# One planned kernel, two sets of ranks: a searched instruction order is replaced by another

## The chip, the cores and the metric

The kernel runs on one core of a Trainium2 chip. The time is device microseconds of one execution of the whole program. A core has engines that run beside each other, each with its own instruction queue that is worked off strictly in order: TensorE (PE, matrix products; its weight loads are listed as PEld), VectorE (DVE), ScalarE (ACT), GpSimd (POOL) and SyncE (SP), which here does nothing but issue transfers from memory. An engine waits for another by a semaphore.

## What is computed

Four layers follow each other over 2048 tokens of width 640: attention A, mixer B, attention A, mixer B, each with a normalization ahead of it and a residual sum. The same weights serve both A layers and both B layers.

```
A: for each of 64 segments of 32 tokens, in order:
     h = [mem (8 rows), normalized segment (32 rows)]
     q, k, v = h Wq, h Wk, h Wv                     # 32 heads of 192
     o = softmax(mask(q k^T / sqrt(192))) v Wo
     mem = o[:8]; out = o[8:]
B: h  = gelu(ln(x) w1), quarters of it shifted by +1, -1, +2, -2 tokens
   x1 = x + h w2;   out = x1 + gelu(ln(x1) w3) w4
```

The memory rows make attention a recurrence: a segment needs the memory that the segment before it left.

## The kernel before

Steps and lanes. The kernel runs both A layers at once. Lane 0 is a segment of the first A layer, lane 1 a segment of the second, five segments behind it (`LAG = 5`). There are 69 steps: steps 0 to 4 have lane 0 alone, 5 to 63 both lanes, 64 to 68 lane 1 alone. In a two-lane step the 2 x 40 rows of the two lanes stand side by side, so that a weight tile that is loaded once serves both. The B layers run in chunks of 64 tokens per lane, one chunk in every two steps, between the operations of the attention steps. A steady pattern is therefore a pair of steps. Most of the weights don't fit on chip and stream in again in every step.

Inside `attention_step` eight groups of four heads go through the same chain. `keys_queries` makes keys (psk) and queries (psq), L943; ScalarE copies the queries (qT, L954), and three copies bring the keys to kT: one by VectorE (L962), and two half-height ones, of which ScalarE has the one and VectorE the other (L969). `attend` then does, by names that the ranks use:

- `fs` (PE, L1059): scores into pss
- `f1` (DVE, L1071): adds the mask and takes the row minimum
- `f2` (ACT, L1078): exponential, into Pm
- `f3` (DVE, L1082, L1083, L1084): sums, reciprocals, the product with them
- `f4` (PE, L1094): transposes of Pm into pst
- `f5` (ACT, L1102): copy to PT
- `f6` (PE, L1111): PT times values, into pso
- `f7` (DVE L1124 and ACT L1122): copies of the two halves of pso to oT

`project` (`f8`, PE, L1146) multiplies each half of oT with Wo and sums into psy over the step. `values3` makes the values (psv, L999), four matmuls of 32 weight columns side by side (the 32-row mode; PE changes into and out of it); ScalarE copies them to V (L979), and `fst` (DVE, L1022) moves parts of V to and from a stash, because in every even step the values of a part of the next step are made too. At the end of a step the memory rows go from psy into the next step's input hT (`fm`, L1173, lane 0 by ScalarE, lane 1 by VectorE), and the other rows into yTB (L1181).

The chunk operations are on VectorE and ScalarE too: residual sums (L1344, L1519, L1626), statistics (L1192 and after), gelu (L1234 to L1247), and copies of transposed tiles; their matmuls are L1443, L1502, L1565 and L1611, their transposes L1216, L1332 and L1339. GpSimd computes the reciprocal roots (L1202, L1383) and moves small pieces and chunk rows.

What sets the order. Nothing is issued in the order in which the functions run. Each calls `add` with an engine, a planned duration, a due time, the function that issues the instructions, and the buffers that it reads and writes. From the buffers `add` makes the edges between operations. It also looks up a rank: `RANK` holds, for each kind of step (`first`, `step0`, `step1`, single-lane kinds with `a` and `b`, `chunk`, `chunk_end` and so on) and for each operation's name, one number for each occurrence; the operation's priority is the time at which its step begins plus this number. `STEP = 48` is the nominal length of a step.

`Plan.place` then places operation after operation. For each engine it takes those that could start within 0.12 us (PE) or 0.05 us (others) of the earliest, and of these the one of the lowest priority; then the engine whose choice starts first. It counts with these lines:

```
free[e] = o.end - (OVER if e in ("ACT", "DVE") else 0.0)
...
elif x.e == e:
    at = o.end
else:
    at = o.end + (PE_LAT if e == "PE" else LAT)
```

`OVER` is by how much an operation on VectorE or ScalarE may start before the end of the one ahead of it, `PE_LAT` and `LAT` are the time from the end of an operation to the start of one on another engine that needs it. Weight loads are in two streams (`wa` for attention, `wb` for the chunks), each sorted by due time, not by rank; both are issued by SyncE. A load for a ring buffer is held until the buffer is free, and many are paced: they wait for a matmul that the plan has finished by then. In the end the operations are issued in the order of the plan, so that each engine's queue has its operations in that order. The planned times themselves don't reach the chip; only the order and the waits do. An operation's waits are made from the tiles that it touches.

Of the kernel before, what the change touches and what calls it, by code (L numbers as in the profile page):

```python
# [21 lines left out]
HG = 4  # L22
# [13 lines left out]
HI = (4.0, 3.0, 0.5)  # L36
# [12 lines left out]
LAT = 0.12  # L49
PACE = 0.25  # L50
OVER = 0.07
PE_LAT = 0.3
# [17 lines left out]
        "apply_ln.f": (25.27, 41.664, -40.648,),  # L70
        "chunk.f1": (45.412,),
        "chunk.f2": (-82.555,),
        "chunk.f3": (3.327,),
        "chunk.fe": (24.593,),
        "chunk.fe3": (21.521,),
        "chunk.fel": (42.947,),
        "chunk.fh": (-0.422,),
        "chunk.fhr": (63.222,),
        "chunk.fhs": (50.947,),
        "chunk.fl": (28.336,),  # L80
        "chunk.fs": (-9.07, 87.616,),
        "chunk.ft": (7.491,),
        "chunk.ftl": (17.084,),
        "chunk.fw": (12.223, 22.504, -3.661, 53.412, 35.584, 12.252, 39.5, 46.586, 6.412, 58.779, 65.304, -26.695,
            70.326,),
        "chunk.fx": (-11.005,),
        "chunk.fx0": (22.308, -12.232,),
        "chunk.fxu": (56.045,),
        "chunk.fz": (56.767,),
        "gelu.f1": (38.422, 8.702, 36.115, -5.73, 21.831, 15.367, 64.826,),  # L90
        "gelu.f2": (43.173, 25.388, 24.176, 19.651, 26.845, 61.238, 13.188,),
        "gelu.f3": (22.801, 11.157, 6.781, 20.622, 53.105, 19.314, 93.475,),
        "gelu.f4": (10.721, 20.836, -33.181, 19.632, -36.914, 31.698, 22.735,),
        "ln_ops.f1": (11.17, 37.33,),
        "ln_ops.f2": (63.628, 7.618,),
        "load_b.fn": (65.723, 2.515, -5.69, 32.658, 14.841, 42.334, 13.103, 39.659, 31.513, 14.364, -26.748,
            28.991, -16.99,),
        "transposes.f": (-36.173, -13.388, 3.992,),
    },
    "chunk_end": {  # L100
        "apply_ln.f": (6.64,),
        "chunk_end.fc": (57.832, 24.612, 4.237,),
        "chunk_end.fs": (38.711, 43.074,),
        "chunk_end.fst": (95.595, 64.015,),
        "chunk_end.fw": (90.265, 22.799, 53.015, 46.575, 23.39, 90.769,),
        "chunk_loads.f": (-2.609, 25.49, 54.721, 25.49, 119.762,),
        "chunk_loads.fz": (93.177, 10.841,),
        "ln_ops.f1": (5.751,),
        "ln_ops.f2": (54.739,),
        "load_b.fn": (20.608, 39.141, 22.427, 3.097, 19.618, 38.065,),  # L110
        "transposes.f": (67.877,),
    },
    "first": {
        "attention_step.attend.f1": (17.516, 11.944, 14.226, 51.703, 15.679, 65.842, 19.995, -4.963,),
        "attention_step.attend.f2": (32.206, 42.804, 35.52, 41.913, -17.146, -14.377, 72.053, -27.992,),
        "attention_step.attend.f3": (-7.419, 21.341, -6.131, 6.53, 64.995, 69.729, 29.276, 10.119,),
        "attention_step.attend.f4": (10.251, 43.894, 9.208, 36.337, -7.089, -6.588, 28.677, 84.166,),
        "attention_step.attend.f5": (14.759, 3.778, -100.306, 53.388, 82.279, 0.476, 47.399, 15.365,),
        "attention_step.attend.f6": (90.867, 51.374, 14.829, -13.387, 17.139, -1.653, -11.48, 21.746,),
        "attention_step.attend.f7": (24.097, 32.506, -26.804, 15.046, 99.332, 15.074, 33.257, 0.473, 24.79, 21.819,  # L120
            44.274, 15.984, 46.8, -11.85, 91.331, -6.294,),
        "attention_step.attend.fs": (60.998, 29.267, -12.034, -20.909, -26.536, 49.498, 35.908, -49.275,),
        "attention_step.fm": (-61.879,),
        "attention_step.fy": (25.64,),
        "attention_step.keys_queries.fk": (17.421, 58.065, 9.482, 20.243, 9.394, -98.29, 7.011, 33.049,),
        "attention_step.keys_queries.fk2": (-4.397, 14.541, 0.117, 21.364, 22.853, -9.996, 51.371, 12.329, -0.942,
            20.9, 57.916, 6.956, 17.166, 53.786, -1.12, 2.359,),
        "attention_step.keys_queries.fn": (-13.958, -17.525, 11.691, -25.108, 33.6, 24.516, -1.859, 18.409, 24.831,
            40.038, -26.96, 38.663, -14.016, -41.294, 98.804, 16.239, -13.809, 19.397, 1.785, 82.684, -31.643,
            20.351, 48.626, 49.47, 62.456, -30.688, -19.311, 32.72, -1.817, -26.25, 56.128, 29.575, -8.583,  # L130
            -17.298, 29.27, 36.05, -13.413, 28.739, 22.805, 44.373, 33.733, 41.172, 59.995, 29.44, 19.316, -14.128,
            -42.971, -21.254, -22.334, 55.507, -26.092, 24.156, 37.618, 13.893, -32.471, -2.697, -8.536, -14.197,
            18.653, 29.426, 82.311, 4.407, 35.396, -56.925,),
        "attention_step.keys_queries.fq": (-13.353, 21.377, 42.471, -2.143, 80.272, 36.699, -4.403, -15.8,),
        "attention_step.project.f8": (37.543, -0.806, 26.185, -3.505, 34.604, 23.024, -14.191, 31.212, 4.164,
            1.038, -3.259, 37.652, -52.502, -35.229, -7.961, 59.829,),
        "attention_step.v_copy.fe": (19.654, -51.565, 21.646, -22.381, 22.407, 6.892, 38.736, 77.812, 14.575,
            -18.961, -28.987, 55.198, 4.611, 56.209, 9.831, 65.23,),
        "attention_step.values.fv": (-17.77, 20.626, 38.167, -40.002, 80.137, 64.626, 30.911, 32.6,),
        "load_pair.fn": (48.935, 59.468, 10.497, 32.661, 50.274, 37.547, 28.935, 9.775, 53.542, 46.99, 40.122,  # L140
            36.648, 112.97, 32.973, -92.931, 33.724, -11.929, -12.279, 42.521, 2.858, 56.922, 37.386, 26.098,
            14.743, 33.522, 13.106, -14.298, 13.674, -8.217, -0.55, 13.502, -8.22, 40.412, 66.89,),
        "res_tile.fn": (116.073, 26.692, 15.064, 6.014, 5.501, 33.759, 3.951, 78.07, 78.067, 29.286, 42.528,
            -1.231, 36.946, 18.179, 12.925, -20.94, 153.972, 45.562, 102.56, 44.042,),
    },
    "last": {
        "apply_ln.f": (15.55, 43.414, 24.403,),
        "chunk.fc2": (-35.922, 69.473,),
        "chunk.fhr": (81.736,),
        "chunk.fs": (16.778, 14.665,),  # L150
        "chunk.ft": (1.105,),
        "chunk.fw": (28.085, -24.907, -12.43, -4.473, 0.43, -1.158, -12.745, -45.377, -28.417, 8.666, 54.761,),
        "chunk.fx": (29.273,),
        "chunk.fxu": (23.382,),
        "chunk.fz0": (131.626,),
        "chunk.halves.fa": (87.746, 5.116,),
        "chunk.halves.fd": (1.941, -19.583,),
        "chunk.halves.fn": (26.898,),
        "gelu.f1": (-43.383, 77.058, 13.807, 6.784, 64.672, 16.189,),
        "gelu.f2": (-32.682, -1.806, -11.508, 4.099, 26.283, -24.627,),  # L160
        "gelu.f3": (51.44, 35.022, 19.314, 63.957, 22.411, 49.713,),
        "gelu.f4": (9.085, 9.082, 68.146, 24.736, 61.493, -21.618,),
        "ln_ops.f1": (-12.151, 16.761,),
        "ln_ops.f2": (19.688, 54.968,),
        "load_b.fn": (10.497, 39.223, 41.188, 36.31, 9.331, -26.904, -11.528, 106.685, 30.89, 11.853, 5.373,
            33.721, 40.049,),
        "transposes.f": (-21.635, 103.144,),
        "warm.fwarm": (34.071, 4.62, -30.566, -28.23, 41.493, 17.753, 22.802, 4.697, -30.894, -0.639, 15.017,
            -26.293, -11.758,),
    },  # L170
    "last_end": {
        "chunk_end.fs": (-1.799, 35.629,),
        "chunk_end.fst": (11.599, -16.415, 45.847, 23.719,),
        "chunk_end.fw": (-3.425, 18.9, -25.169, 39.823, 36.518, -23.839, 8.894, 1.265,),
        "load_b.fn": (27.538, 83.834, 26.762, 26.765, 24.871, 14.264,),
    },
    "start": {
        "apply_ln.f": (16.824,),
        "chunk_loads.f": (93.18, 44.689, 6.824,),
        "ln_ops.f1": (1.076,),  # L180
        "ln_ops.f2": (57.543,),
        "start.f1": (15.362,),
        "start.f2": (-2.19,),
        "start.f3": (-11.851,),
        "start.f4": (-11.213,),
        "start.f5": (34.327, 11.809, -2.229, 11.05,),
        "transposes.f": (31.955,),
# [408 lines left out]
def kernel(  # L596
# [296 lines left out]
    def attention_step(t):  # L893
# [88 lines left out]
        def values3(i_, pr, s0, wbs, wv):  # L982
# [33 lines left out]
            for j in range(2) if ahead_v or behind_v else ():  # L1016
# [7 lines left out]
                if behind_v:  # L1024
                    add("DVE", 0.46, s0, fst, r=(B("stash", pr, j),), w=(B("V", j, "s"),))
                else:
                    add("DVE", 0.46, s0 + 0.2, fst, r=vk_, w=(B("stash", pr, j),))
# [744 lines left out]
```

## Time and profile before

| | |
|---|---|
| median of 3 runs | 3314.65 us (3310.34 to 3320.3) |
| profiled execution, its own time | 3318.65 us |
| its span, first to last instruction | 3316.5 us |
| mean granted TensorE clock | 0.990 |
| busy: PE, PEld, DVE, ACT, POOL | 96%, 85%, 70%, 57%, 7% |
| from memory | 817.14 MB read, 248 GB/s over the span |

The span parts into three: about 256 us until the first two-lane step (of which the first step takes 89 us), 59 two-lane steps at 95.5 us a pair, and about 239 us for the five last steps and the last chunk. These come from the times of the copies at the end of each step (L1181).

How to read the profile: a row of a group names line, engine, operation and tiles. A busy share is that of the whole span. In the waits, `A <- B: total, times, longest` says that the engine of A sat idle until B had ended, in us. In a timeline row the columns are start, length, engine, line, operation, tiles and shapes, count, and in brackets the idle time ahead of it and what ended it. In windows the columns are the stretch, its length, the busy time of PE, PEld, DVE, ACT and POOL with instruction counts, the granted clock, the busy share of DMA and its GB/s. Records of matmuls overlap: each is some 200 ns long while they follow each other at a fraction of that. "Cover" in what follows is the PE work that stands in PE's queue between a matmul and a later one that needs its result through other engines.

### The profile page before, as it was taken

Reading aid. Unit: us, or ns where it says so; the run is one execution under the profiler, and the core shown is the slowest. Engines: PE = TensorE matmul, PEld = TensorE weight load, DVE = VectorE, ACT = ScalarE, POOL = GpSimd, SP = SyncE. Lnnn points to the kernel's source line nnn. Section 1 sums busy time; section 2 is a strip of 40 time slices with the busy share of each in tenths; the row PEclk is TensorE's granted clock in tenths of the full one; section 3 lists DMA queues with packets and bytes.
Section 4 is the critical chain, followed back from the end, with each engine's and each line's share of the span. In section 5 each row is a group of like instructions: output and inputs, shape, how many; then the busy total and the mean of one; then the engine's idle time right before and its main releaser. Section 6 shows DMA issues by size and latency. Waiting matters only on the chain.

```text
span 3316.5 us, 173787 instructions
## 1 busy us (share of the span) xinstructions
PE 3183.1 (96%) x77339; PEld 2809.2 (85%) x77341; DVE 2329.5 (70%) x7320; ACT 1898.7 (57%) x4837; POOL 235.1 (7%) x483
## 2 busy tenths in 40 slices
PE   6899999999999999999999999999999999999997
PEld 4778888888888888888888888888888888888875
DVE  2666777777777777777767777677777777777665
ACT  2346666666565666665656666565666655666443
POOL 0000000000000000000000000000000000000000
PEclk7999999999999999999999999999999999999999
DMA  9787778777877777777778777877777777778885
GB/s 374 263 275 246 235 242 267 237 234 252 270 233 238 263 248 232 238 264 259 236 235 273 236 228 251 268 237 236 262 247 234 236 263 254 236 238 271 277 268 198
DMA packets 409752, 833.66 MB, mean 251 GB/s; under 512 B 39680, under 2 KB 207311, under 8 KB 409000
## 3 DMA queue, kind: packets, MB, share of 16 engines
q1 hardware_dynamic: 401704, 809.47, 72.8%
q0 software_dynamic: 7136, 13.00, 1.3%
q8 instruction: 605, 9.91, 1.2%
q14 instruction: 147, 1.20, 0.1%
q10 hardware_dynamic: 160, 0.08, 0.0%
HBM read 817.14 MB, written 5.24 MB: 248 GB/s over the span
## 4 chain that ended last, share of the span: by engine, by line
PE 71%; DVE 20%; DMA 3%; issue 3%; ACT 2%; SPq 0%; POOL 0%; ACTq 0%; DVEq 0%; POOLq 0%
PE psy L1146 15%; PE psk L943 14%; PE psq L943 13%; PE psv L999 10%; PE pss L1059 3%; PE pso L1111 3%; PE y L1611 3%; PE pst L1094 3%; DVE Pm L1084 2%; DVE sm L1082 2%; DVE oT L1124 2%; PE psh L1565 2%; DVE kT L962 2%; DVE st L1192 2%; DVE pss L1071 2%
## 5 line engine op out<-in xcount | busy, mean ns | idle before, releaser
L943 PEld LDWEIGHTS <-wst 128*128 128x128 bf16 x19872 | 804.2, 99 | 78.5 <-issue 62.1
L1146 PE MATMUL psy<-oT,wo 128*128 128x80 bf16 (+1 forms) x16560 | 701.8, 200 | 33.3 <-DVE oT L1124 11.3
L1146 PEld LDWEIGHTS <-wo 128*128 128x128 bf16 x16560 | 631.6, 99 | 75.5 <-issue 63.6
L979 ACT CAST V<-psv 96x384 bf16<-96x384 f32 (+3 forms) x1264 | 583.1, 473 | 119.2 <-PE psv L999 54.5
L943 PE MATMUL psq<-hT,wst 128*128 128x80 bf16 (+1 forms) x9936 | 530.2, 200 | 4.9 <-DMA wst<-in_A_Wq_dram 3.8
L943 PE MATMUL psk<-hT,wst 128*128 128x80 bf16 (+1 forms) x9936 | 503.6, 200 | 18.4 <-DVE hT L1173 14.9
L999 PEld LDWEIGHTS <-hT 128*32 128x32 bf16 (+1 forms) x11840 | 294.9, 96 | 154.2 <-issue 0.4
L954 ACT CAST qT<-psq 128x480 bf16<-128x480 f32 (+1 forms) x552 | 290.5, 526 | 174.0 <-PE psq L943 158.3
L1124 DVE CAST oT<-pso 128x240 bf16<-128x240 f32 (+1 forms) x552 | 213.9, 387 | 229.0 <-ACT oT L1122 145.9
L962 DVE CAST kT<-psk 128x320 bf16<-128x320 f32 (+1 forms) x552 | 256.3, 464 | 129.9 <-ACT kT L969 82.8
L1078 ACT ACTIVATE Pm<-pss,sm 80x320 bf16<-80x320 f32 (+2 forms) x552 | 277.7, 503 | 118.6 <-DVE sm L1071 102.1
L999 PE MATMUL psv<-wv,hT 128*32 128x384 bf16 (+1 forms) x5920 | 343.9, 328 | 0.0
L999 PE MATMUL psv<-wst,hT 128*32 128x384 bf16 x5920 | 341.8, 326 | 0.0
L969 ACT CAST kT<-psk 64x160 bf16<-64x160 f32 (+1 forms) x552 | 151.9, 275 | 314.9 <-PE pss L1059 170.8
L943 PE MATMUL psq<-hT,wq 128*128 128x80 bf16 (+1 forms) x6624 | 322.3, 200 | 8.1 <-DMA wq<-in_A_Wq_dram 5.9
L1102 ACT COPY PT<-pst 80x320 bf16<-80x320 bf16 (+2 forms) x552 | 222.1, 402 | 188.5 <-PE pst L1094 176.2
L943 PE MATMUL psk<-hT,wk 128*128 128x80 bf16 (+1 forms) x6624 | 322.0, 200 | 4.1 <-issue 2.6
L1122 ACT CAST oT<-pso 128x240 bf16<-128x240 f32 (+1 forms) x552 | 189.3, 343 | 210.4 <-PE pso L1111 164.1
L1082 DVE TENSOR_REDUCE sm<-Pm 80x4 f32<-80x320 bf16 (+2 forms) x552 | 250.5, 454 | 64.3 <-ACT Pm L1078 57.3
L969 DVE CAST kT<-psk 64x160 bf16<-64x160 f32 (+1 forms) x552 | 174.3, 316 | 158.5 <-ACT kT L969 89.9
L1071 DVE CUSTOM_DVE_ANT_1 pss<-pss,mask 80x320 f32<-80x320 f32 (+2 forms) x552 | 256.6, 465 | 34.5 <-PE pss L1059 26.1
L943 PEld LDWEIGHTS <-wq 128*128 128x128 bf16 x6624 | 270.5, 99 | 10.1 <-DMA wq<-in_A_Wq_dram 6.3
(140 smaller groups left out, 4290.9 us busy)
## 6 DMA issues: line engine op xcount, KB each, us to landing
wst<-in_A_Wk_dram SPq DMA_DIRECT2D x556, 384.0 KB, 4.8
wst<-in_A_Wq_dram SPq DMA_DIRECT2D x556, 384.0 KB, 4.9
wst<-in_A_Wv_dram SPq DMA_DIRECT2D x418, 384.0 KB, 4.8
wstB<-in_B_w_dram SPq DMA_DIRECT2D x495, 320.0 KB, 4.7
wstB<-in_B_w_dram SPq DMA_DIRECT2D x132, 160.0 KB, 4.1
wo<-in_A_Wo_dram SPq DMA_DIRECT2D x8, 960.0 KB, 12.3
wv<-in_A_Wv_dram SPq DMA_DIRECT2D x2, 1536.0 KB
xw<-in_A_x_dram POOLq DMA_DIRECT2D x31, 80.0 KB, 4.1
```

The costliest lines, as they stand in the source:

```text
L943: nc.tensor.matmul(out=o[:, cc, 0:W], lhsT=wv(kc, GW * j + cc * P, GW * j + (cc + 1) * P), rhs=h[:, kc, cw:cw + W], start=begin(pq), stop= ...
L954: nc.scalar.copy(out=qT[:, :, c0:c0 + N], in_=T(pq)[:, :, off:off + N])
L962: nc.vector.tensor_copy(out=k4[:, :, 0::3, c0:c0 + N], in_=p4[:, :, 0::2, off:off + N])
L969: copy(out=k4[r0:r1, :, jj, c0:c0 + N], in_=p4[r0:r1, :, 1, off:off + N])
L979: (nc.vector.tensor_copy if e == "DVE" else nc.scalar.copy)(out=v_part(*dst), in_=a_)
L999: nc.tensor.matmul(out=o[32 * u:32 * u + n3, :], lhsT=left[:, kc, 32 * g3:32 * g3 + n3], rhs=wv(kc, a, a + GWH), start=(kc == 0), stop=(kc ...
L1071: nc.vector.tensor_tensor_reduce(out=o, in0=o, in1=maskt.unsqueeze(1).to_broadcast([NR, HG, N]), scale=-scale, scalar=3.0e38, op0=ALU.add, ...
L1078: nc.scalar.activation(out=Pb[0:NR, :, 0:N], in_=o, func=ACT.Exp, bias=sm_[0:NR, 0:1], scale=-1.0)
L1082: nc.vector.tensor_reduce(out=sm_[0:NR, 2:2 + HG], in_=Pb[0:NR, :, 0:N], axis=AX.X, op=ALU.add)
L1102: nc.scalar.copy(out=Pt[0:KV, :, 0:N], in_=T(pst)[0:KV, :, c0:c0 + N])
L1124: nc.vector.tensor_copy(out=o_[:, 0:3, off:off + N], in_=T(pso)[:, 0:3, 0:N])
L1146: nc.tensor.matmul(out=o[:, m, cw:cw + W], lhsT=wo[:, cc, m * P:(m + 1) * P], rhs=o_[:, cc, 0:W], start=st, stop=True, skip_group_check=True)
```

## The change

Every rank is replaced: 1932 numbers, of which the old ones lie between −135 and 154 and the new ones between −43 and 223. Priorities are compared with each other alone, so a shift of all of them means nothing. With the ranks, three of the planner's constants and two planned durations change. No function that issues instructions is changed: matmuls, copies, tiles, buffers and loads are the same in kind, size and number. What changes is the order on each engine, which buffer of a ring an operation gets, and at which matmul a paced load is released.

```diff
-LAT = 0.12
+LAT = 0.07
 PACE = 0.25
-OVER = 0.07
-PE_LAT = 0.3
+OVER = 0.0
+PE_LAT = 0.22
...
     "step0": {
-        "attention_step.attend.f4": (-11.674, 5.55, 39.318, 42.365, -14.824, 23.202, -14, 21.737,),
+        "attention_step.attend.f4": (93.018, 31.753, 97.145, 90.514, 98.439, 35.95, 102.186, 69.713,),
...
-        "attention_step.attend.f6": (11.693, 3.676, -24.619, 12.445, 10.497, 41.3, 53.094, -33.164,),
+        "attention_step.attend.f6": (68.624, 56.479, 80.149, 68.079, 79.183, 82.088, 32.809, 24.345,),
...
-                    add("DVE", 0.46, s0, fst, r=(B("stash", pr, j),), w=(B("V", j, "s"),))
+                    add("DVE", 0.43, s0, fst, r=(B("stash", pr, j),), w=(B("V", j, "s"),))
...
-                    add("DVE", 0.46, s0 + 0.2, fst, r=vk_, w=(B("stash", pr, j),))
+                    add("DVE", 0.43, s0 + 0.2, fst, r=vk_, w=(B("stash", pr, j),))
...
-            add("DVE", dve_us(HG * N) + 0.02, hi - HI[0], f1, r=(pss,), w=(pss, smk))
+            add("DVE", dve_us(HG * N) + 0.09, hi - HI[0], f1, r=(pss,), w=(pss, smk))
```

All other lines of the diff are further ranks of this form, in all twelve kinds of step.

## The prediction

> **What bounds the kernel now.** I read the page's busy shares first, then one steady stretch by windows, then the waits, and last the timeline at the places where TensorE pauses.
>
> ```profile
> PE 3183.1 (96%) x77339; PEld 2809.2 (85%) x77341; DVE 2329.5 (70%) x7320; ACT 1898.7 (57%) x4837; POOL 235.1 (7%) x483
> PE psy L1146 15%; PE psk L943 14%; PE psq L943 13%; PE psv L999 10%; PE pss L1059 3%; PE pso L1111 3%; PE y L1611 3%; PE pst L1094 3%; DVE Pm L1084 2%; DVE sm L1082 2%; DVE oT L1124 2%; PE psh L1565 2%; DVE kT L962 2%; DVE st L1192 2%; DVE pss L1071 2%
> ```
>
> TensorE (PE) sets the time: its matmuls lead the chain that ended last, and VectorE (DVE) takes some 20% of it. The change alters no instruction's work, so only PE's pauses can move. How large are they? The next rows are one pair of two-lane steps, cut from one pair's first key matmul to the next pair's.
>
> ```profile
> 1259.95:1355.47 95.52, 93.93 (x2277) 83.60 (x2277) 69.62 (x217) 58.11 (x144) 6.94 (x14) 1.00 0.74 247
> 1355.47:1450.95 95.48, 93.87 (x2282) 83.57 (x2281) 69.81 (x218) 58.09 (x144) 6.95 (x14) 1.00 0.74 247
> ```
>
> The clock is already 1.00, and DMA is 74% busy. Busy time hides short pauses, because each matmul's record is some 200 ns long while one follows another every 36 ns (80 columns), 56 ns (128) or 136 ns (320). So I took start-to-start distances in the timeline and subtracted these paces. The first pair loses 2.93 us: 0.68 where the step pair begins; 1.33 ahead of the transposes of the softmaxed scores, L1094 (0.31, 0.09, 0.27, 0.57, 0.09); 0.88 ahead of output projections, L1146 (0.12, 0.22, 0.13, 0.41); 0.04 elsewhere. There are 59 two-lane steps, so 29.5 pairs and about 86 us, the most that any order of them could win. The largest transpose pause, on VectorE's queue:
>
> ```profile
> 1336.65 0.33 DVE L969 CAST kT<-psk 64x160 bf16<-64x160 f32 x1 [0.43 <-ACT kT L969]
> 1337.01 0.49 DVE L1071 CUSTOM_DVE_ANT_1 pss<-pss,mask 80x320 f32<-80x320 f32 x1
> 1337.53 0.08 DVE L1071 DVE_READ_ACCUMULATOR2_ANT sm<- 80x1 f32 x1
> 1337.53 0.49 DVE L1626 SCALAR_TENSOR_TENSOR vbg<-y,xw 128x320 bf16<-128x320 f32 x1
> 1338.04 0.42 DVE L1022 COPY V<-stash 32x384 bf16<-32x384 bf16 x2
> 1338.49 0.41 DVE L1124 CAST oT<-pso 128x240 bf16<-128x240 f32 x1
> 1338.93 0.49 DVE L1626 SCALAR_TENSOR_TENSOR vbg<-y,xw 128x320 bf16<-128x320 f32 x1
> 1339.34 0.47 DVE L1082 TENSOR_REDUCE sm<-Pm 80x4 f32<-80x320 bf16 x1
> ...
> 1340.06 0.49 DVE L1084 TENSOR_TENSOR Pm<-Pm,sm 80x320 bf16<-80x320 bf16 x1
> ```
>
> The mask-and-minimum (L1071) is done at 1337.6. The sum (L1082) that the exponential feeds starts only at 1339.34, behind 1.8 us of foreign work in the queue, and PE pauses until L1084 is through. So a steady pause is a matter of what stands in VectorE's queue. The waits show a second one:
>
> ```profile
> DVE oT L1124 <- ACT oT L1122: 145.9, 94, 4.0
> DVE kT L969 <- ACT kT L969: 89.9, 137, 6.2
> DVE kT L962 <- ACT kT L969: 82.8, 96, 2.1
> ```
>
> Two halves of one tile are copied by two engines, and one half waits for the other, though neither needs the other's data. The planner has no such edge.
>
> **The accounts against the trace.** Old: hand-off 0.12, from PE 0.3, and 0.07 of overlap between queued operations. New: 0.07, 0.22, 0. Trace: ScalarE (ACT) and VectorE start 33 ns after the other's end; PE starts 53 ns after theirs; after PE's last matmul start they begin at 240 ns, which less its 36 ns is 0.205. So the new latencies are nearer. For the overlap I set a page against the row. The Trainium skill (VectorE: DVE Perf Modes, "The DRAIN you can't avoid") says that the next operation does not start until the pipe is empty, while an unheld one starts earlier. In the trace about half of the queued, unchained VectorE operations start some 80 ns before their predecessor's record ends (1339.34 against 1338.93 + 0.49), the others 13 to 34 ns after it; the mean over all successors is 19 ns early. I take 0.02 for each. The old 0.07 undercounted a nearly full queue, the new 0 overcounts it a little. By the page, a window of 15 to 19 operations costs 0.3 to 0.4 us more than by the row.
>
> **The change, part by part.** I set the two built programs' queues beside each other, engine by engine. Matmuls and copies are the same in number and size; both orders enter or leave the 32-row value mode 16 times in a steady pair, at about 0.1 us each. In the single-lane ends the new order does so 16 times more: +1.6 us. The duration edits (0.43 for 0.46, +0.09 for +0.02) are planner numbers and issue nothing.
>
> *Step boundary.* In both orders the last projection is followed at once by the next pair's keys, which need the memory columns: 0.205 + ACT copy 0.19 + 0.03 + DVE copy 0.20 + 0.05 = 0.68. It stays. The transposes L1332 stand only three key operations later now; in the timeline their input's copies end 0.44 us after the boundary, against 0.65 us of keys: covered.
>
> *Softmax transposes.* For each I compared the DVE work queued between an earlier DVE operation and L1084, plus 0.26 of hand-offs, with the PE work standing between that operation's matmuls and the transpose. A deficit is a window that is overdrawn; each is counted alone, so they don't add. In the old order the same five transposes at which the trace pauses come out overdrawn (0.30, 0.92, 0.80, 0.32, 0.90), and one more by 0.1 to 0.2. In the new order the worst is 0.03, the next have 0.08 to 0.13 to spare. Moving foreign DVE work thus covers them, barely. The window contains no ACT waits like the 0.43 us above. Ends: 0, all 1.33 gone, to 1.3, ACT waits bring it back. I take 0.30, near the windows.
>
> *Projections.* Attention output (L1111) is copied in halves, DVE 0.407 and ACT 0.358, and the projection of a half follows. Here a rule speaks against the change. The Trainium skill (PSUM — Partial Sum Buffer, "PSUM bank collisions raise a hardware error") says that the compiler back end adds a dependency between any two instructions on different engines in one bank and quadrant, "ACT↔DVE too". The rows above agree, and here it reaches PE:
>
> ```profile
> 1276.62 0.36 ACT L1122 CAST oT<-pso 128x240 bf16<-128x240 f32 x1 [0.20 <-DVE oT L1124]
> ...
> 1277.03 0.70 PE L1146 MATMUL psy<-oT,wo 128*128 128x80 bf16 x15
> ```
>
> By the planner a half needs 0.205 + 0.407 + 0.053 = 0.67; chained, the second needs 0.205 + 0.358 + 0.034 + 0.407 + 0.053 = 1.06. The smallest covers in the old order are 0.84, 0.86, 0.86, 0.86, 0.90, two short, by 0.22 and 0.07. The shorter latencies let the new planner set projections closer: 0.54, 0.56, 0.68, 0.72, 0.72. With the copying order of the program, six are short: 0.34, 0.34, 0.20, 0.08, 0.06, 0.06, in all 1.08. Of the 0.88 measured now, 0.29 is of this kind and the rest is queue. Ends for the new: 0.2 (pauses elsewhere open the gap first) to 1.5 (queue too). I take 0.90.
>
> *Values after the transposes.* The copy PT (0.421, so 0.68 with hand-offs) had at least 0.86 of PE work over it, now 0.82; ACT's queue can add. Ends 0 to 0.8; I take 0.20.
>
> *Loads and GpSimd.* Order within each weight stream stays, the streams interleave anew, and waits for PE pace the issue. The shortest time from the PE work that releases a load to its use falls from 5.8 to 5.05 us, once a pair; landing took 3.1/4.8/15.4 us (min/median/max). That load comes after a gap in the queue, so nearer 3.1: 0 taken, up to 1 us a pair if late, and the loads behind it on SP's queue would then be late as well. GpSimd's steps (rsqrt 0.6, history copies 0.2) have microseconds of cover in both orders: 0.
>
> *Sum for a pair.* 0.68 + 0.30 + 0.90 + 0.20 + 0.05 = 2.13 against 2.93: −0.80, times 29.5 = −24 us.
>
> *The ends.* The first step takes 89 us and loads at 364 GB/s with DMA 0.99 busy; loads keep their order: 0. Single-lane steps lose 5 to 6 us each. Direct needs over cover, old to new: opening four steps, projections 4.8 to 7.1, softmax 2.8 to 1.2; closing five, projections 4.8 to 4.2, softmax 2.4 to 1.4, PT 1.0 to 2.2. These nearly cancel (together +0.2); queue windows there improve as in the pair. I take −7, and with +1.6 for mode changes −5 (−15 to +8).
>
> In all −29: the profiled execution, 3318.65 (span 3316.5 and 2.15 around it), becomes about 3290. It lies 4 us above the median of the runs, 3314.65, which becomes **3286**. The main case's own range is 3270 to 3302.
>
> **Rivals.** *The chain takes it all (slower).* If kT and oT halves that wait for ACT block VectorE's queue, the softmax windows, with about 0.1 us to spare, are overdrawn again. Price: softmax 1.3, projections 1.3, PT 0.25, boundary 0.68: 3.53 a pair, +0.60 × 29.5 = +18, and no gain at the ends: about 3333. It decides once softmax pauses exceed 1.1 us a pair. For it: 145.9 + 89.9 + 82.8 us of such waits. Against: most fall where VectorE had time, and the old order has them too.
>
> *Both queues clear (much faster).* Projection gaps are absorbed and softmax is clean: 0.68 + 0.1 + 0.3 + 0.1 = 1.2 a pair, −1.75 × 29.5 = −51, ends −10: about 3254. For it: no overdrawn windows. Against: copy order is fixed in the program, so the chained 1.06 is due each time.
>
> *No effect.* Pauses move from transposes to projections one for one: 2.9 a pair, 3315. The window counts speak against it.
>
> *A late load.* One late load a pair at 0.5 to 1 us: +15 to +30 on the main case, 3300 to 3316.
>
> **How the numbers follow.** Main case 0.46, much faster 0.21, slower 0.18, no effect 0.07, late load 0.08. 3314.65 ± 0.3% is 3305 to 3325, about what a measurement of this kernel can tell from no change. Faster: 0.46 + 0.21 + a quarter of the late load, plus a few hundredths lost from the main case's edge: 0.67. Same: 0.07 + most of the late load = 0.15. Slower 0.18. The range from 3245 to 3325 takes the faster rival and no effect whole; outside it lie most of the slower case and little else.
>
> **What would show it.** Right: a steady pair of about 94.7 us; pauses ahead of L1094 near 0.3 us a pair; pauses ahead of L1146 as large as before or larger, after an oT half that waited for the other engine; the boundary at 0.68. Wrong: transposes that pause over 1 us a pair behind kT waits, or PE waiting for wst.

## The result

The changed kernel takes 3293.43 us (median of 4 runs, 3290.41 to 3296.21), the kernel before 3315.55 (4 runs, 3310.34 to 3320.3). The ratio is 0.9933, with a 95% interval of 0.9915 to 0.9952: 22 us faster. The profiled execution took 3296.21 us, with a span of 3294.5 against 3316.5.

Where did the 22 us of span come from? Cut at the copies that end each step (L1181), they part so: 3.3 up to the end of step 5, 14.6 in the 58 two-lane steps after it (2772.6 to 2758.0, or 95.61 to 95.10 us a pair), 4.1 in the closing part. The last of these is not shown to come from the order. In step 67 the granted clock was 0.96 in the kernel before and 1.00 in the changed one; in two runs below with the old order (e3 and e6), where it was 1.00 through all of the single-lane steps at the end, the closing part took 232.5 and 231.5 us, less than the changed kernel's 234.6 and the 238.6 before. The two-lane steps ran at 1.00 in both.

Two steady pairs of the changed kernel, of which the first is the first one shown before, by windows:

```profile
1253.16:1348.07 94.91, 93.82 (x2278) 83.64 (x2278) 70.79 (x217) 58.33 (x144) 6.99 (x14) 1.00 0.76 249
967.25:1062.32 95.07, 93.86 (x2278) 83.61 (x2277) 70.73 (x217) 58.33 (x144) 6.93 (x14) 1.00 0.76 248
```

Instructions, clock and DMA share are as before; a pair is some 0.5 us shorter, although VectorE is busy some 1 us longer with the same 217 instructions.

To see which pauses went, I aligned TensorE's instructions with the order of the plan and took, for steps 6 to 63, every start-to-start distance less the pace of the matmul (the paces of the prediction). The means per pair, in us, for all kernels that ran:

| | softmax L1094 | projections L1146 | values L1111 | boundary | chunk transposes, matmuls | keys, queries | all pauses of a pair | opening and closing single-lane steps, all nine |
|---|---|---|---|---|---|---|---|---|
| before | 1.34 | 1.05 | 0 | 0.68 | 0.16 | 0.15 | 3.51 | 70.3 |
| after | 0.33 | 1.11 | 0.43 | 0.68 | 0.05 | 0.23 | 3.02 | 62.2 |
| e1_half_first | 0.74 | 0.26 | 0.66 | 0.68 | 0.11 | 0.23 | 3.06 | 61.8 |
| e8_unchained | 0.15 | 0.30 | 0.63 | 0.68 | 0.05 | 0.27 | 2.45 | 62.7 |
| e9_chain_order | 0.18 | 0.44 | 0 | 0.68 | 0.04 | 0.41 | 2.15 | 60.6 |
| e10_before_chain_order | 0.84 | 0.62 | 0 | 0.68 | 0.14 | 0.19 | 2.66 | 70.3 |
| e3_before_move | 0.96 | 1.07 | 0 | 0.68 | 0.59 | 0.21 | 3.65 | 69.1 |
| e6_before_less | 1.08 | 1.07 | 0 | 0.68 | 0.09 | 0.21 | 3.26 | 69.6 |
| e7_after_less | 0.33 | 1.11 | 0.40 | 0.68 | 0.07 | 0.14 | 2.98 | 64.6 |
| e4_old_ranks_new_account | 1.05 | 3.07 | 2.40 | 1.37 | 1.57 | 0.64 | 10.9 | 88.7 |

The column of all pauses also has what lies inside a group of matmuls or ahead of scores (0.1 to 0.4 us, 0.8 in e4). The last column is in us for all nine steps together, and a lower granted clock counts in it as pauses. The table closes: after against before, 0.49 us × 29.5 + 8.1 = 22.6 us, and the span fell by 22.0. The softmax gave up 1.01 us a pair. Half of that came back: 0.43 ahead of the products with the values, where nothing had paused before, and the rest in keys, in projections and inside groups.

What the new order does with VectorE's work is seen at the place of the largest pause before, where two residual sums (L1626) stood between the mask and the softmax's sums. Both now stand behind the softmax's product, and TensorE does not pause ahead of these transposes:

```profile
1331.80 0.49 DVE L1084 TENSOR_TENSOR Pm<-Pm,sm 80x320 bf16<-80x320 bf16 x1
1332.31 0.89 DVE L1626 SCALAR_TENSOR_TENSOR vbg<-y,xw 128x320 bf16<-128x320 f32 x2
```

The chain that ended last shows the same from another side. By engines, before and after:

```profile
PE 71%; DVE 20%; DMA 3%; issue 3%; ACT 2%; SPq 0%; POOL 0%; ACTq 0%; DVEq 0%; POOLq 0%
PE 89%; DMA 3%; DVE 3%; ACT 3%; issue 1%; SPq 0%; POOL 0%; ACTq 0%; POOLq 0%; DVEq 0%
```

VectorE's share of it was 20% before. It is 3% now, and the time fell by 0.67%. A share of the chain counts all work that lies on it, also where another engine's queue is only a short pause ahead. The pauses say what can be won, the share doesn't.

What took the place of the old pauses? ScalarE's waits for its copy of keys in the kernel before:

```profile
ACT kT L969 <- DVE kT L969: 20.9, 89, 0.9
ACT kT L969 <- DVE kT L962: 2.0, 8, 0.3
```

And the waits of the changed kernel:

```profile
DVE oT L1124 <- ACT oT L1122: 241.5, 234, 2.2
ACT kT L969 <- DVE kT L962: 87.1, 183, 1.0
DVE kT L969 <- ACT kT L969: 69.5, 134, 2.6
DVE kT L962 <- ACT kT L969: 11.7, 15, 3.8
```

The wait of VectorE's half copy for ScalarE's rose from 145.9 us to 241.5. ScalarE's copy of keys waited for one of VectorE's 97 times and 22.9 us before; now it waits 183 times and 87.1 us, always for the copy of full height. VectorE's waits for ScalarE's in turn fell, in that copy from 82.8 us to 11.7. Both changes reach TensorE. One of the two largest projection pauses of the pair, in the timeline:

```profile
1328.41 0.36 ACT L1122 CAST oT<-pso 128x240 bf16<-128x240 f32 x1 [0.33 <-PE pso L1111]
1328.81 0.41 DVE L1124 CAST oT<-pso 128x240 bf16<-128x240 f32 x1 [2.05 <-ACT oT L1122]
...
1329.27 0.52 PE L1146 MATMUL psy<-oT,wo 128*128 128x80 bf16 x10 [0.17 <-DVE oT L1124]
```

VectorE idled 2.05 us, of which the last 0.4 with its input ready, since ScalarE read the same bank first; the projection that stands first in TensorE's queue needs VectorE's half. The pause of TensorE there, start to start, is 0.34 us. The pair has another of 0.34, and five of 0.19 to 0.04. And the new pause ahead of the values:

```profile
1323.02 0.29 ACT L969 CAST kT<-psk 64x160 bf16<-64x160 f32 x1 [0.35 <-DVE kT L962]
1323.33 0.47 ACT L979 CAST V<-psv 64x384 bf16<-64x384 f32 x1
...
1323.82 0.42 ACT L1102 COPY PT<-pst 80x320 bf16<-80x320 bf16 x1
...
1324.29 0.45 PE L1111 MATMUL pso<-PT,V 80*128 80x80 bf16 x8 [0.16 <-ACT PT L1102]
```

ScalarE sits idle for 0.35 us, because VectorE reads the key bank first. Behind its key copy stand a copy of values and PT, and TensorE waits for PT.

### The profile page after: what moved, and what is told of

Its sections match the earlier page's. It is cut to its first block, busy times and chain, and to the rows that moved or that the text cites. A ratio compares the mean times of both kernels' runs of the same rounds, so it can differ in the third digit from the quotient of the medians.

```text
span 3294.5 us, 173909 instructions
## 1 busy us (share of the span) xinstructions
PE 3178.7 (96%) x77339; PEld 2809.6 (85%) x77341; DVE 2361.9 (72%) x7320; ACT 1908.4 (58%) x4837; POOL 235.5 (7%) x483
## 4 chain that ended last, share of the span: by engine, by line
PE 89%; DMA 3%; DVE 3%; ACT 3%; issue 1%; SPq 0%; POOL 0%; ACTq 0%; POOLq 0%; DVEq 0%
PE psy L1146 17%; PE psk L943 17%; PE psq L943 16%; PE psv L999 15%; PE pso L1111 5%; PE pss L1059 4%; PE psh L1565 3%; PE y L1611 3%; PE pst L1094 3%; PE psv L1039 2%; PE psh L1443 1%; DMA wst<-in_A_Wq_dram 1%; PE hs L1502 1%; DMA wst<-in_A_Wk_dram 1%; DVE oT L1124 1%
## 5 line engine op out<-in xcount | busy, mean ns | idle before, releaser
L943 PEld LDWEIGHTS <-wst 128*128 128x128 bf16 x19872 | 820.6, 99 | 51.9 <-issue 28.0
L1146 PE MATMUL psy<-oT,wo 128*128 128x80 bf16 (+1 forms) x16560 | 703.1, 200 | 30.5 <-DVE oT L1124 12.3
L1146 PEld LDWEIGHTS <-wo 128*128 128x128 bf16 x16560 | 637.8, 99 | 68.9 <-issue 50.6
L943 PE MATMUL psk<-hT,wst 128*128 128x80 bf16 (+1 forms) x9936 | 514.3, 200 | 19.7 <-DVE hT L1173 14.9
L1124 DVE CAST oT<-pso 128x240 bf16<-128x240 f32 (+1 forms) x552 | 214.0, 388 | 280.9 <-ACT oT L1122 241.5
L999 PE MATMUL psv<-wv,hT 128*32 128x384 bf16 x5920 | 344.2, 328 | 0.1
L943 PEld LDWEIGHTS <-wk 128*128 128x128 bf16 x6624 | 267.5, 99 | 11.8 <-issue 11.7
L1084 DVE TENSOR_TENSOR Pm<-Pm,sm 80x320 bf16<-80x320 bf16 (+2 forms) x552 | 255.7, 463 | 29.7 <-DVE sm L1083 0.5
```

What stands on the lines that cost most here:

```text
L943: nc.tensor.matmul(out=o[:, cc, 0:W], lhsT=wv(kc, GW * j + cc * P, GW * j + (cc + 1) * P), rhs=h[:, kc, cw:cw + W], start=begin(pq), stop= ...
L999: nc.tensor.matmul(out=o[32 * u:32 * u + n3, :], lhsT=left[:, kc, 32 * g3:32 * g3 + n3], rhs=wv(kc, a, a + GWH), start=(kc == 0), stop=(kc ...
L1084: nc.vector.tensor_tensor(out=Pb[0:NR, :, 0:N], in0=Pb[0:NR, :, 0:N], in1=sm_[0:NR, 6:6 + HG].unsqueeze(2).to_broadcast([NR, HG, N]), op=A ...
L1124: nc.vector.tensor_copy(out=o_[:, 0:3, off:off + N], in_=T(pso)[:, 0:3, 0:N])
L1146: nc.tensor.matmul(out=o[:, m, cw:cw + W], lhsT=wo[:, cc, m * P:(m + 1) * P], rhs=o_[:, cc, 0:W], start=st, stop=True, skip_group_check=True)
```

## Experiments

Two theories stood against each other on each side. For the gain: VectorE's queue ahead of the softmax (windows), or something else that came with the order. For what still pauses: the chain of two engines that read one bank, as a local shortage that one can mend at the place, or as a price that only changes hands. e1, e9, e8 and e10 ask about the chain; e3, e6 and e7 about the windows; e4 about the account.

### The half that is needed first is copied first

```diff
-    placed = plan.place()
+    placed = first_half_first(plan.place())
...
+        need = {id(o): min(at[id(s)] for s in o.succ if s.e == "PE" and s.fn.__qualname__.endswith("f8")) for o in (x, y)}
+        a, b = (x, y) if need[id(x)] < need[id(y)] else (y, x)
...
+        if not any(o.e == a.e or a in o.succ for o in between):
+            order.insert(j, order.pop(i))
...
```

The copies' place in the program decides which of them waits; no engine's own queue changes.

> The changed kernel; in 197 places the two copies of an attention output are issued in the other order, so that the half whose projection stands first in TensorE's queue is copied first and the other one waits. Every engine's own queue is unchanged. Theory A, the shortage is local: in a steady pair the projections fall short of their chained needs by 1.08 us together, and with the copies turned by 0.14. So the 1.11 us that projections pause fall to about 0.2, 0.9 us a pair, times 29.5 = 27 us: about 3267, and a pair of 94.1. Theory B, the chain only changes hands: a copy that waits holds up its whole queue (ScalarE's, or VectorE's with the softmax behind it), and the pauses come back ahead of other projections, transposes or scores: 3288 to 3298, with the pauses of a pair still near 3.0 us in sum.

Measured: 3291.91 us (4 runs), ratio to before 0.9933 (0.9916 to 0.9949), the changed kernel's own ratio. Theory A is right at the place and wrong in the sum. The projections' pauses fell from 1.11 us a pair to 0.26, as worked out; 0.41 came back ahead of the softmax transposes, 0.23 ahead of the values, 0.13 inside the scores. The projection shown above no longer pauses:

```profile
1326.43 0.41 DVE L1124 CAST oT<-pso 128x240 bf16<-128x240 f32 x1 [1.23 <-PE pso L1111]
...
1326.87 0.36 ACT L1122 CAST oT<-pso 128x240 bf16<-128x240 f32 x1 [0.77 <-DVE oT L1124]
...
1326.95 0.70 PE L1146 MATMUL psy<-oT,wo 128*128 128x80 bf16 x15
```

But elsewhere in the pair the same turn does this:

```profile
1262.71 0.36 ACT L1122 CAST oT<-pso 128x240 bf16<-128x240 f32 x1 [0.54 <-DVE oT L1124]
...
1262.96 0.28 ACT L969 CAST kT<-psk 64x160 bf16<-64x160 f32 x1
...
1263.28 0.49 DVE L962 CAST kT<-psk 128x320 bf16<-128x320 f32 x1 [0.61 <-ACT kT L969]
...
1265.43 0.32 PE L1094 MATMUL pst<-ident,Pm 80*128 80x80 bf16 x4
```

ScalarE's half now waits for VectorE's, so its key copy comes later; VectorE's own key copy waits for that; the sums and the product of the softmax stand behind it, and TensorE pauses 0.29 us ahead of the transposes. In the changed kernel ScalarE went first here and these transposes did not pause. So the chain has two cascaded links, oT and kT, and it closes a loop between the two queues. A choice by the nearest projection alone does not see the second queue.

### The chain's order set place by place

```diff
-    placed = plan.place()
+    placed = chain_order(plan.place())
...
+TURN = {
+    ('kT', 'step1'): (0, 0, 1, 2, 0, None, None, 0),
+    ('oT', 'step1'): (1, 0, None, 1, 0, 1, 1, 0),
...
+        new = g if v is None else dve[:v] + act + dve[v:]
+        for p, q in zip(new, new[1:]):
+            edge(p, q)
```

`TURN` says for each kind of step and each of its eight groups how many of VectorE's copies come before ScalarE's. The values were chosen by walking through both orders' queues with the lengths and hand-offs of the trace. Every engine keeps its own order; the operations are issued in an order that obeys the new edges.

> The changed kernel; 278 of its 1104 groups of copies out of one bank (the two of an attention output, the three of a key tile) are chained in another order: which engine reads the bank first is set for each place in a step with the lengths and hand-offs of the trace, for projections, transposes and values together and not for the nearest projection alone. Every engine's own queue is unchanged. If the order of the chain is what still costs: the 1.11 us of projections and the 0.43 us ahead of the products with the values fall to about half, 0.7 us a pair, times 29.5 = 21 us, so 3272, at best 3260. If the chain's cost is the same whichever engine goes first (one of the two always waits 0.36 to 0.44 us): 3288 to 3298.

Measured: 3268.43 us (3266.59 to 3272.97, 4 runs), ratio to before 0.9867 (0.9852 to 0.9882). It is the fastest kernel here: 45 us below the one before (3313.20 in these runs) and 23 below e1 on the same chip. The pauses of a pair fell from 3.02 us to 2.15: projections by 0.67, values by 0.43, softmax by 0.15; some 0.4 of that came back ahead of keys and queries and inside groups of matmuls, from causes that were not looked into. The values' 0.43 is gone, here at one of its two places in the pair:

```profile
1277.60 0.28 ACT L969 CAST kT<-psk 64x160 bf16<-64x160 f32 x1
...
1277.91 0.49 DVE L962 CAST kT<-psk 128x320 bf16<-128x320 f32 x1 [0.51 <-ACT kT L969]
1278.39 0.42 ACT L1102 COPY PT<-pst 96x320 bf16<-96x320 bf16 x1
...
1279.31 0.46 PE L1111 MATMUL pso<-PT,V 96*128 96x80 bf16 x8
```

Here ScalarE takes the keys first and VectorE, which has the time, waits. In the changed kernel VectorE went first at this place, ScalarE's copy waited for it, and TensorE paused 0.09 us for PT. At the other place, that of the pause shown above (0.32 us), the turn is the same: ScalarE's key copy starts at 1313.27, VectorE's after an idle time of 0.99 us at 1313.59, and TensorE does not pause. One of two readers always waits, as the expectation's second half says; but who waits decides whether TensorE does. The total of the oT waits is even larger than in the changed kernel (115.1 + 176.6 us against 241.5 + 30.5), while the pauses are smaller. The pair of copies that e1 spoiled is left with ScalarE first here, and the pair of the 0.34 us pause is turned as in e1. The keys' order was not run without that of the attention outputs, so their shares are not measured apart.

### The chain taken away

```diff
-                            nc.scalar.copy(out=o_[:, 3:6, off:off + N], in_=T(pso)[:, 3:6, 0:N])
+                            nc.scalar.copy(out=o_[:, 3:6, off:off + N], in_=qT[:, 3:6, off:off + N])
...
-                    add("ACT" if hf else "DVE", (act_us if hf else dve_us)(3 * N), hi - HI[0], f7, r=(pso,), w=(oks[hf],))
+                    add("ACT" if hf else "DVE", (act_us if hf else dve_us)(3 * N), hi - HI[0], f7, r=(pso,), w=(oks[hf],), after=(last_op["pso"],) if hf else ())
```

> The changed kernel; ScalarE's half copy of each attention output takes the same 3 x 80 columns from a tile in on-chip memory (qT) and no longer from the bank that VectorE's half copy reads; it still waits for the last product with the values. So the two copies no longer touch one bank and neither waits for the other. Half of each attention output is not the computed one. If that chain is what TensorE pays for: both halves are then due after 0.67 us; against the covers 0.54, 0.56, 0.68, 0.72, 0.72 only 0.24 us a pair is short where 1.08 was, and VectorE's queue no longer stands still behind ScalarE: 0.8 to 1.0 us a pair, times 29.5 = 24 to 30 us less than the changed kernel, 3264 to 3270, the waits of the one copy for the other gone from the trace. If the pauses are the queues' own (the copies stand behind other work): 3285 to 3295.

Measured: 3275.49 us (3271.76 to 3278.49, 4 runs), ratio to before 0.9882 (0.9866 to 0.9897); 18 us below the changed kernel's 3293.43. The waits of the two copies for each other are gone from the trace, and the projections' pauses fell to 0.30, against the 0.24 that was worked out. So the first theory holds in kind: it is the shared bank that the projections pay for. The time lies 5 us above its range. The values pause 0.63 instead of 0.43, 6 us over the 29.5 pairs, behind copies of keys that this kernel leaves chained, and 0.18 a pair came inside groups and ahead of scores, about as much as the softmax gave up. ScalarE's copy also takes 390 ns, where it took 358 from the bank:

```profile
L1122 ACT COPY oT<-qT 128x240 bf16<-128x240 bf16 x472 | 184.1, 390 | 154.2 <-PE pso L1111 147.5 <-PE psk L943 0.4
```

### The same for the kernel before

The edit is that of the second experiment, with a table for the old order.

> The kernel before, old ranks and account; 200 of its 1104 groups of copies out of one bank are chained in another order, chosen for each place in a step as in the changed kernel's version of this. Every engine's own queue is unchanged. If what the chain costs and what the ranks win are separate: before loses by the chain about as much as after, 0.8 us a pair, 20 to 25 us, so about 3290, and the gap between the two ranks stays at about 20. If the old order's pauses are mostly work queued on VectorE (softmax 1.34 us a pair, only 0.29 us of the projections' shortage is the chain's): at most 10 us, 3303 to 3315.

Measured: 3291.32 us (3289.54 to 3292.85, 4 runs), ratio to before 0.9930 (0.9915 to 0.9945), so 22 us faster than before. The first theory holds. The four times make a square: old ranks 3313, new 3293; with the chain set, 3291 and 3268. The ranks win 20 to 23 us with or without the chain, and the chain 22 to 25 with or without the new ranks. My expectation's second branch was wrong about the old order: a chain also held up VectorE ahead of its softmax. L1094's pauses fell from 1.34 to 0.84 us a pair, the largest of them, the 0.57 of the prediction, to 0.14.

### One operation moved in the old order

```diff
-    placed = plan.place()
+    placed = move_foreign(plan.place())
...
+    for x in [o for o in placed if o.e == "DVE" and o.fn.__qualname__.endswith("chunk_end.<locals>.fs")]:
...
+        j = next((k for k in range(i + 1, len(order)) if order[k].e == "DVE"), None)
+        if j is None or not order[j].fn.__qualname__.endswith("attend.<locals>.f3"):
+            continue
...
+        order.insert(j, order.pop(i))
```

> The kernel before; one of VectorE's operations moves by one place, 30 times: the second residual sum of a chunk (L1626, 0.49 us) goes behind the sums and the product of the softmax (L1082 to L1084) that it stood ahead of. Window theory of the prediction: foreign work in VectorE's queue is what holds up the transposes, so the steady pause of 0.57 us ahead of that transpose falls to about 0.1: 0.47 us a pair, times 29.5 = 14 us, 3302. Rival: the pause goes to the transposes of the chunk (L1216) that need the moved sum, or to the next window, since the queue is as full as before: 3310 to 3322.

Measured: 3319.55 us (10 runs), ratio to before 1.0023 (1.0013 to 1.0032): no gain, 6 us slower. The rival holds. The transposes L1094 paused 0.38 us a pair less; L1216 and the rest of the chunk paused 0.43 more:

```profile
1342.94 0.48 DVE L1626 SCALAR_TENSOR_TENSOR vbg<-y,xw 128x320 bf16<-128x320 f32 x1
1343.07 0.21 PEld L1094 LDWEIGHTS <-Pm 80*128 80x128 bf16 x4 [0.19 <-DVE Pm L1084]
...
1346.00 0.45 DVE L1208 TENSOR_SCALAR h2u<-vbg,st 128x640 bf16<-128x640 bf16 x1 [0.21 <-POOL st L1202]
...
1346.50 0.28 PEld L1216 LDWEIGHTS <-h2u 128*128 128x128 bf16 x5 [0.19 <-DVE h2u L1208]
```

The moved sum starts a chain of its own: statistics, GpSimd's root, the normalization, the transposes L1216. It has a deadline as near as the softmax's. So pushing "foreign" work behind what waits did not help by itself. In the changed kernel the same sum does stand behind the softmax, but there the other places on the queues are new too.

### Work taken out, in both orders

```diff
             def fs(op, k=k):
                 cs = slice(HC * k, HC * (k + 1))
+                if k and not last:
+                    nc.vector.memset(xo[:, cs], 0.0)
+                    return
```

> The kernel before; the second residual sum of a chunk (L1626, 0.49 us, once in a steady pair, in the overdrawn window ahead of a softmax transpose) is left out and a memset of the same 320 columns stands in its place (estimate 0.1 to 0.2 us), so half of every chunk's output is zero. Window theory: 0.3 to 0.4 us less work in VectorE's queue, and nothing that comes later instead, so that much less pause in every pair: 9 to 12 us, 3301 to 3304. Rival, other waits take the place: less than 4 us, 3309 to 3315.

> The changed kernel with the same sum left out for a memset, half of every chunk's output being zero. Window theory: in the new order the windows of the softmax have the room for VectorE's foreign work, so taking 0.3 to 0.4 us out of one of them wins nothing or little: 0 to 3 us, 3289 to 3293. Rival, VectorE's queue sets the pauses in the new order as in the old: 9 to 12 us, 3281 to 3284.

Measured: in the old order 3304.20 us, ratio 0.9969 (0.9954 to 0.9984), so 8.9 us less; in the new order 3294.07, ratio to before 0.9945 (0.9930 to 0.9960), against 0.9933 for the changed kernel: nothing. In the profile of e6 the memset takes 192 ns where the sum took 488, so 0.30 us left VectorE's queue, 33 times: 9.8 us. The old order pays for most of it: the 58 two-lane steps took 6.6 us less (2766.0), where some 8.7 left the queue, and the interval of the runs allows 5 to 15 us. In the new order, where the sum stands behind the softmax's product, it costs nothing: 2757.8 us against 2758.0. That is the window theory from both sides, for this one operation.

### Old ranks under the new account

```diff
-LAT = 0.12
+LAT = 0.07
 PACE = 0.25
-OVER = 0.07
-PE_LAT = 0.3
+OVER = 0.0
+PE_LAT = 0.22
```

and the two planned durations of the change, in the kernel before.

> The kernel before with its old ranks, and with the three constants and the two planned durations of the changed kernel. If the account that is nearer to the trace brings the gain by itself, this order is about as fast as the changed kernel's: 3285 to 3300. If ranks are good only together with the account under which they were searched (a rank names a place between neighbours that stand elsewhere now): slower than before by over 1%, 3350 to 3430.

Measured: 3569.10 us (2 runs), ratio 1.0773 (1.0751 to 1.0794): 256 us slower, worse than I had put the bad case. Pauses rose from 3.51 us a pair to 10.9, in every class, and a second step boundary in each pair now costs its 0.68. The chain by engines:

```profile
PE 64%; DVE 15%; ACT 7%; DMA 4%; issue 3%; POOL 0%; ACTq 0%; DVEq 0%; POOLq 0%
```

An account that is nearer to the trace brings nothing by itself. A rank is a number in a competition among operations that are ready at the same time; another account makes others ready, and the old numbers no longer pick what they were searched to pick. As far as this run goes, the gain belongs to ranks and account together. Which of the three constants does the damage, and whether the new ranks lose as much when one of them is turned back, wasn't tried.

## Why the prediction was right, and where it was off

The time was put at 3286 us and is 3293, inside the main case's own range; the direction and the steps hold, with one term too small. Part of the closeness is luck. The pairs gave 14.6 us where 24 were forecast; the ends gave 7.4 where 5 were, and 4.1 of these are not shown to come from the order.

- *What bounds.* Right: TensorE's pauses moved, and the table of pauses gives the change of span within 1 us. The prediction's own pair lost 2.93 us; the mean over all pairs is 3.51, with more ahead of projections (0.17) and ahead of chunk transposes, keys and queries (some 0.3) than the sampled one had. A pair after the change was forecast at 2.13 and loses 3.02; that most of this stands in both orders, and so drops out of the difference, is luck of the sample.
- *Boundary*, 0.68: right, unchanged to the hundredth.
- *Softmax transposes*, 0.30 taken: 0.33 measured. Counting the work in VectorE's queue against TensorE's cover was the right step, and e6 and e7 bear it out for one operation. The size itself was taken between 0 and 1.3 without a sum behind it, so that it was met so closely is in part luck. What the step left out is that ScalarE's waits fill these windows too: e10 lowers the old order's pause with no VectorE work moved.
- *Projections*, 0.88 to 0.90 a pair: 1.05 to 1.11 in the mean over all pairs, and 0.03 more inside. The six places named short, 1.08 in all, are what is paid: the pair shown has two of 0.34 and one of 0.19, and e1 lifts that shortage to 0.14 and the pauses there fall by 0.85. By the rule of the Trainium skill (PSUM — Partial Sum Buffer, "PSUM bank collisions raise a hardware error"), the compiler back end puts two engines that touch one bank and quadrant one after the other, which by the lengths in the trace made the second half due after 1.06 us and not the planner's 0.67. The runs agree: with the bank no longer shared (e8), 0.30 of the 1.11 is left.
- *Values after the transposes*, 0.20 taken of 0 to 0.8: 0.43. This is the term that was mis-sized. "ACT's queue can add" was the right sentence; I had not looked for what stands on that queue ahead of PT. It is ScalarE's key copy that waits for VectorE's: 22.9 us of such waits before, 87.1 now.
- *Sum for a pair*, −0.80: −0.49 over steps 6 to 63. Of the 0.31 missing, about 0.23 is the values, 0.07 the projections, 0.08 keys and queries and 0.02 the softmax; the chunk gave 0.11 back.
- *Ends*, −5: −7.4 by the cuts, −8.1 by the pauses, of which only the opening's 3.3 are clear of the clock: the old order took 304.7 us to the end of step 5 in e6 too, where the clock was higher than before, against the changed kernel's 301.7.
- *DRAIN.* For the overlap I took the row (about half of the successors start 80 ns early) rather than what the Trainium skill says first (VectorE: DVE Perf Modes, "The DRAIN you can't avoid"), that the next operation waits for an empty pipe. By that, the old windows would have been overdrawn by 0.3 to 0.4 us more; e6 returned 6.6 of 8.7 us in the two-lane steps, which both readings allow, so no run here decides what the windows cost.
- *Loads.* TensorE's waits for streamed key and query weights grew from 4.4 us in the whole program to 7.0, where the late-load rival needs 15 to 30 more.

Of the rivals, *both queues clear* did not come, but e9 shows that a part of it was there to be had: 2.15 us a pair with the same ranks, where the rival put 1.2. The reason given against it, that the order of the copies is fixed in the program, was the right one, and it is also the lever. *The chain takes it all* was a fair warning: its mechanism, copies that wait for ScalarE and block VectorE's queue, is what e1 sets off. It stayed below its point of decision: softmax pauses were 0.33, and 0.74 in e1, against the 1.1 that it needs.

## What to carry to other kernels

Where two engines read one bank, the order in which the program issues the two reads is a schedule decision like any other: choose it place by place, by which of the two queues has time to wait, and count what stands behind the waiting copy and not only the copy's own consumer. Before trusting a gain from moving one operation in a full queue, look for the chain that the moved operation starts; taking the work out for one run tells whether that work, at that place, costs time at all. And don't change a planner's costs under priorities that were searched with the old ones: here costs nearer to the trace, with the old priorities, made the kernel 256 us slower.

## What the runs showed of the hardware that I had not expected

- Two copies out of one bank waited for each other even where they read different rows: VectorE's half-height key copy (rows 64 to 128) for ScalarE's of rows 0 to 64, 134 times and 69.5 us in the changed kernel. The two also write one tile, kT, and the trace doesn't say who made the dependency; that the bank is the reason is shown by e8 for the halves of oT alone.
- For ScalarE, the bank that TensorE writes was not the slower source: a copy of 128x240 took 358 ns from it in f32 (the changed kernel), and 390 ns from on-chip memory in bf16 (e8). Source and type differ at once, so the two are not told apart.
